# Two experts of a mixture in early and late passes, and TensorE's order in these passes written out

## The chip, the cores and the metric

One Trainium2 chip, one of its cores. The metric is the device time of the kernel in microseconds (us), the median over runs. The engines are called by their short names: PE (TensorE; PEld is its weight load), DVE (VectorE), ACT (ScalarE), POOL (GpSimd) and SP (SyncE, which issues most DMAs).

## The reference

The kernel computes an attention layer with a memory term and then a mixture of experts on its output. Shapes: batch B = 4, heads H = 8, sequence S = 576, head size D = 64, so 2304 tokens of width 512; E = 8 experts with hidden width 1024; float32.

```python
scores = scale * np.matmul(q, k.transpose(0, 1, 3, 2))      # causal mask, softmax
local = np.matmul(a, v)
q_p = phi(q)                                                # elu + 1
mem_out = einsum(q_p, M_prev) / (einsum(q_p, z_prev) + 1e-06)
x = (g * mem_out + (1 - g) * local), as (B * S, H * D)
...
noisy_logits = x @ w_gate + np.log1p(np.exp(x @ w_noise)) * noise
top2 = np.argpartition(-noisy_logits, 2, axis=1)[:, :2]     # weights: softmax over the two
for e in range(E):
    for k in range(2):
        mask = top2[:, k] == e
        h = np.maximum(x[mask] @ w1[e], 0.0)
        out[mask] += top2_w[mask, k, None] * (h @ w2[e])
```

Each token goes to two of the eight experts, and which ones is known only after its attention output has been computed.

## The kernel before

**Attention and routing.** attention() works through 20 chunks (4 batches of 5 chunks: four of 128 tokens and one of 64). The finished rows of x go to the DRAM scratch xall (line 643). For each chunk xt_logits (line 142) makes the gate's logits in three steps, f1 (transposes on PE), f2 (products) and f3 (transpose back). For each batch routing (line 176) yields a list of small steps on DVE and ACT; one of them, count, makes M, the mask of chosen experts, and places (line 237) counts positions with small matmuls on PE. A token's place gives its slot: every expert owns CAP = 608 slots. put (line 280) writes the token's row (token number, other slot, weight) into the DRAM table tab with an indirect DMA on POOL, two for each chunk. The last batch is routed in two parts, chunks 0 to 2 and 3 to 4; its tokens get slots from EARLY = 384 on (the offset dl, line 251), so the first 384 slots of every expert hold only tokens of batches 0 to 2. What is left of the routing when attention ends comes back as the list tail (line 797); its last step is rounds.

**Early rows of expert 0.** early() (line 837) runs when batch 2 has been routed: SP loads the first 384 rows of expert 0's part of tab into tabE, after all puts so far (line 842), and POOL gathers the 384 rows of x into xgE (line 850). xprep (line 852) turns such a tile on PE, and ACT and DVE split it into a high and a low part, xT.

**Experts.** All products run as three matmuls of split operands (high x high, high x low, low x high). Per expert there are 8 steps f of 128 hidden units. mm1 (line 907) makes the hidden tile for a step, with the relu on ACT (hTh, line 922) and the low part on DVE (hTl, line 923); mm2 (line 927) adds the step to the output banks y, one for each tile of slots: tiles 0 to 2 have 128 slots, tiles 3 and 4 have LATE = 112. Weights of a step are loaded by SP (load_w, lines 870 and 871, 2 x 256 KB, four buffers) and split by split_w (line 874): w1h on DVE, w1l on POOL (line 881), w2h on ACT, w2l on DVE. In the loop over steps, first(k + 1), the mm1 of the next step, comes ahead of the mm2 of step k.

The list of passes (line 945) sets the order: expert 0 with tiles 0 to 2 (early), expert 0 with tiles 3 and 4 (late; five of its eight steps take up splits that are still there: the order turn0 and the dict again), then experts 1 to 7 with all five tiles. In pass 0 the steps of tail are mixed in (tails) and the last puts go out, two after each step. When both lists are empty, load_tab (line 895) loads the whole table into tall, after all puts, and POOL gathers the late rows of expert 0 (xload(1)), which xprep turns on PE at the end of pass 0 (line 1074), ahead of pass 1.

From expert 1 on the rows of x are turned by DMA: xload gathers a tile into xg (five buffers), turn_x (line 996) separates the two 16-bit halves into pl (two buffers) with two copies on DVE and issues two DMA transposes on SP into trn; turned (line 1006) joins the halves on ACT and splits them into xT on ACT and DVE. xslot (line 1025) says in which step this is done: one tile a step in pass 1, joined four steps later.

**Results.** finish (line 1042) scales a tile by the routing weight. Rows of expert 0 are stored to the DRAM scratch ybuf only. For a later expert, yload gathers for each slot the row that the token's other expert has put there, if it had a lower number (g, with a memset on POOL ahead, line 814); finish adds it on DVE in one instruction, SP stores the sum to ybuf, and POOL scatters it to out (line 823). Such POOL and SP work is taken from the queue pq, two or three items a step.

**What sets the order.** The framework's planner orders the instructions of each engine anew, from the order in which they are written, with its own model of their durations; engines execute their queues in order. issue_after holds an instruction back behind another one. in_turn (line 726) fixes the order of the PE instructions that its function emits, behind those emitted by the one before; attention's steps all go through it, the experts' don't. The loop at line 1131 for more than CAP tokens of one expert runs zero times here.

Of the kernel before, what the change touches and what calls it, by code (L numbers as in the profile page):

```python
# [9 lines left out]
F32 = mybir.dt.float32  # L10
# [9 lines left out]
P = 128  # L20
# [26 lines left out]
def tile_attention_moe(ctx: ExitStack, tc: tile.TileContext, q, k, v, M_prev, z_prev, beta,  # L47
# [269 lines left out]


    def attention():
        with ExitStack() as c2:  # L320
# [405 lines left out]
            def in_turn(f):  # L726

                traced = nc.cur_bb.bb.instructions
                n_ = len(traced)
                f()  # L730
                for x_ in nc.cur_bb.bb.instructions[n_:]:
                    if x_.engine == mybir.EngineType.PE:
                        if "pe" in R:
                            tc.add_manual_dep(x_, R["pe"].name, mybir.DependencyInfo(
                                mybir.DependencyClass.NoSync, mybir.DependencyReason.DATA), reason="order of the steps")
                        R["pe"] = x_

            for u in range(NU + 2):
# [44 lines left out]
                for y, f in enumerate(ys):  # L783
                    in_turn(f)
                    if small:
                        in_turn(small.popleft())
                    while done * ny < (y + 1) * nx:
                        in_turn(xs[done])
                        done += 1
                        if small:  # L790
                            in_turn(small.popleft())
# [38 lines left out]
    tabE = ep.tile([P, 3, 4], I32, name="tabE")  # L830
# [6 lines left out]
    def early():  # L837
# [4 lines left out]
        after_puts(nc.sync.dma_start(out=tabE, in_=tab[0:EARLY].rearrange("(p t) c -> p t c", p=P)))  # L842
# [5 lines left out]
        for t in range(3):  # L848
            nc.vector.memset(R["xgE"][t], 0.0)
            gather_x(R["xgE"][t], tabE[:, t, 0:1], (B - 1) * S)  # L850
# [35 lines left out]
    def experts(tail):  # L886
        with ExitStack() as c3:
# [5 lines left out]
            tall = mp.tile([P, E, NT, 4], I32, name="tall")  # L893
# [13 lines left out]
            def mm1(ws, xT, tiles, odd=0):  # L907
# [5 lines left out]
                else:  # L913
                    cols = [(0, EARLY, "ab"[odd]) if tiles[0] < 3 else (EARLY, CAP, "ab"[1 - odd])]
                hp = [ps_h.tile([P, 512], F32, tag="h" + n_, name="h" + n_)[:, 0:c1_ - c0_] for c0_, c1_, n_ in cols]
                for c in range(4):
                    for i_, (w_, xi) in enumerate(((h1, 0), (h1, 1), (l1, 0))):
                        for (c0_, c1_, _), o in zip(cols, hp):
                            nc.tensor.matmul(o, w_[:, c, :], xT[xi][:, c, c0_:c1_],  # L919
# [25 lines left out]
            passes = [(0, [0, 1, 2]), (0, [3, 4])] + [(e, [0, 1, 2, 3, 4]) for e in range(1, E)]  # L945
# [10 lines left out]
            def tails(n):  # L956
                done = 0
                while done < n and tail:
                    if done and getattr(tail[0], "pe", False):
                        return  # L960
                    tail.popleft()()
                    done += 1

            def wload(k_):
                if k_ < len(steps) and k_ not in wr and k_ not in again:
                    p, f = steps[k_]
                    wr[k_] = load_w(mp, passes[p][0], turn0[f] if p == 1 else f, "m", 4)
# [7 lines left out]
            def first(k_):  # L975
                p, f = steps[k_]
                HT[k_] = mm1(ws[k_], XT[p], passes[p][1], f % 2 if p < 2 else 0)
# [3 lines left out]
            def xload(p):  # L981
# [4 lines left out]
                def one(t):  # L986
                    g = mp.tile([P, DM], F32, tag="xg", name="xg", bufs=5)
                    XG[p, t] = g
                    if len(XG) <= 5:
                        with tc.issue_after(R["hl"].ins):  # L990
                            nc.vector.memset(g, 0.0)
                    gather_x(g, tall[:, e, t, 0:1])
# [3 lines left out]
            def turn_x(xg, t):  # L996
# [5 lines left out]
                tr = R["turn", t] = mp.tile([P, 2, 4, P], U16, tag="trn", name="trn", bufs=4)  # L1002
# [3 lines left out]
            def turned(xT, t):  # L1006

                tr = R["turn", t]
# [4 lines left out]
                a_, b_ = slots_of(t)  # L1013
# [4 lines left out]
            def yload(p, t):  # L1018
                e = passes[p][0]
                g = mp.tile([P, DM], F32, tag="g", name="g", bufs=5)  # L1020
                G[p, t] = g
                with tc.issue_after(R["w1l"].ins):
                    gather_y(g, tall[:, e, t, 1:2], e * CAP)

            def xslot(p, f):

                if p == 0 and f + 3 >= NF:
                    p, f = 1, f - NF
                if p == 0 or p + 1 == NP_:
                    return  # L1030
                nx_ = passes[p + 1][1]
                begin = {1: [0, 1], 2: [2], 3: [3], 4: [4]} if p > 1 else {t - 3: [t] for t in range(5)}
# [175 lines left out]
```

## Time and profile before

| what | us |
|---|---|
| median of 3 runs | 771.13 |
| the three runs | 771.13, 771.33, 764.79 |
| profiled execution, first to last instruction (span) | 745.5 |
| what the median lies above that span | 25.6 |
| PE busy in the span | 700.6 (94%) |
| DVE, ACT, POOL busy | 422.5, 374.4, 347.3 |

The profiled execution's own time is known as its span only; the difference to the runs holds what lies around the span, and the scatter of runs. A profile counts an engine busy while an instruction runs; matmuls are pipelined, so their times overlap and the distance between starts is what a matmul costs. In the rows of stages below the columns are: the stage, its length, then for PE, PEld, DVE, ACT and POOL the busy time and in brackets the count of instructions, then the clock granted to PE as a share of full speed, the busy share of the DMA engines, and GB/s. In rows in order of time a bracket at the end is the engine's idle time just before, and what ended it.

### The profile page before, as it was taken

The numbers are of one execution on the slowest core, as the hardware profiler recorded it, in microseconds if no ns is written. First come the engines' busy times: TensorE is split into PE (matmuls) and PEld (weight loads), VectorE is DVE, ScalarE is ACT, GpSimd is POOL, SyncE is SP. The second block draws the span as 40 slices with busy tenths as digits, with TensorE's granted clock in tenths as the row PEclk, the third lists the DMA queues.
The fourth block names the chain that finished last, engine by engine and source line by source line (L and its number), as shares of the span: only waits on it lengthen the run. The fifth ranks groups of instructions, "written<-read, shape, count | busy, mean of one in ns | idle before, by whom it ended". The sixth has DMA issues, their size and how long they took to land. (4 is left out here: it accounts for less than half of the span.)

```text
span 745.5 us, 14446 instructions
## 1 busy us (share of the span) xinstructions
PE 700.6 (94%) x5166; PEld 603.4 (81%) x5166; DVE 422.5 (57%) x1073; ACT 374.4 (50%) x963; POOL 347.3 (47%) x368
## 2 busy tenths in 40 slices
PE   6999899999999878889999999999999999999993
PEld 4778777877878767777998898889889988988892
DVE  3766587678677669445555454455455354554312
ACT  4787788788888753155244153253153162253110
POOL 6513424632862516464533843833834744615402
PEclk7899999999999999989999999999999999999997
DMA  8764332251310047496593593684694695755201
GB/s 159 107 135 94 90 95 52 64 115 45 83 39 30 3 129 188 103 210 185 121 209 105 154 212 117 163 195 134 178 193 142 176 190 164 184 120 176 63 0 64
DMA packets 165919, 92.95 MB, mean 125 GB/s; under 512 B 110564, under 2 KB 145380, under 8 KB 165840
## 3 DMA queue, kind: packets, MB, share of 16 engines
q1 hardware_dynamic: 155760, 72.97, 40.5%
q0 software_dynamic: 10080, 18.98, 10.2%
q8 instruction: 43, 0.70, 0.4%
q14 instruction: 36, 0.29, 0.1%
HBM read 69.68 MB, written 22.54 MB: 124 GB/s over the span
## 5 line engine op out<-in xcount | busy, mean ns | idle before, releaser
L881 POOL TENSOR_TENSOR w1lm<-w1sm,w1hm 128x512 fp32r<-128x512 f32 x63 | 81.8, 1300 | 131.1 <-DVE w1hm L880 72.2
L932 PE MATMUL y<-w2hm,hTh 128*128 128x512 f32 (+1 forms) x310 | 122.9, 397 | 0.0
L932 PE MATMUL y<-w2hm,hTl 128*128 128x512 f32 (+1 forms) x310 | 122.4, 395 | 0.0
L932 PE MATMUL y<-w2lm,hTh 128*128 128x512 f32 (+1 forms) x310 | 122.0, 394 | 0.0
L922 ACT ACTIVATE hTh<-ha 128x304 fp32r<-128x304 f32 (+2 forms) x64 | 27.2, 426 | 157.1 <-PE ha L919 156.9
L882 ACT CAST w2hm<-w2sm 128x512 fp32r<-128x512 f32 x65 | 40.2, 620 | 102.1 <-PE y L932 102.1
L559 ACT ACTIVATE a<-sc,nb 128x128 f32<-128x128 f32 (+4 forms) x160 | 82.6, 531 | 11.4 <-DVE nb L538 6.7
L538 DVE TENSOR_REDUCE nb<-sc 128x1 f32<-128x384 f32 (+4 forms) x128 | 70.2, 557 | 27.7 <-PE sc L534 17.1
L883 DVE TENSOR_TENSOR w2lm<-w2sm,w2hm 128x512 fp32r<-128x512 f32 x65 | 49.0, 754 | 55.2 <-ACT w2hm L882 55.2
L880 DVE CAST w1hm<-w1sm 128x512 fp32r<-128x512 f32 x65 | 30.2, 464 | 78.3 <-PE hb L919 53.2
L919 PE MATMUL hb<-xTh,w1hm 128*128 128x304 f32 (+1 forms) x236 | 71.8, 304 | 0.0
L919 PE MATMUL ha<-xTl,w1hm 128*128 128x304 f32 (+1 forms) x236 | 71.8, 304 | 0.0
L919 PE MATMUL ha<-xTh,w1hm 128*128 128x304 f32 (+1 forms) x236 | 71.5, 303 | 0.0
L919 PE MATMUL ha<-xTh,w1lm 128*128 128x304 f32 (+1 forms) x236 | 71.1, 301 | 0.0
L919 PE MATMUL hb<-xTl,w1hm 128*128 128x304 f32 (+1 forms) x236 | 71.1, 301 | 0.0
L919 PE MATMUL hb<-xTh,w1lm 128*128 128x304 f32 (+1 forms) x236 | 70.8, 300 | 0.0
L932 PEld LDWEIGHTS y<-w2hm,hTl 128*128 128x128 f32 (+1 forms) x310 | 56.9, 184 | 15.6 <-DVE hTl L923 0.2
L932 PEld LDWEIGHTS y<-w2lm,hTh 128*128 128x128 f32 (+1 forms) x310 | 57.1, 184 | 12.1
L932 PEld LDWEIGHTS y<-w2hm,hTh 128*128 128x128 f32 (+1 forms) x310 | 57.0, 184 | 11.3
L577 PE MATMUL tpa<-identr,a 128*128 128x128 f32 x400 | 59.2, 278 | 5.1 <-ACT ll L170 3.4
L1001 DVE COPY pl<-xg 128x512 uint16<-128x512 uint16 x70 | 41.4, 639 | 38.1 <-DMA trn<-pl 26.2
L578 ACT COPY aT<-tpa 128x512 f32<-128x512 f32 x120 | 57.6, 519 | 6.4 <-PE tpa L577 4.4
(252 smaller groups left out, 1634.8 us busy)
## 6 DMA issues: line engine op xcount, KB each, us to landing
w1sm<-in_moe_w_dram SPq DMA_DIRECT2D x65, 256.0 KB, 3.2
w2sm<-in_moe_w_dram SPq DMA_DIRECT2D x65, 256.0 KB, 3.4
y_scratch<-o SPq DMA_DIRECT2D x21, 256.0 KB, 3.4
vt<-in_v_dram SPq DMA_DIRECT2D x16, 256.0 KB, 4.2
xall_scratch<-xr SPq DMA_DIRECT2D x16, 256.0 KB, 2.2
kn<-in_k_dram SPq DMA_DIRECT2D x15, 256.0 KB, 3.5
qn<-in_q_dram SPq DMA_DIRECT2D x15, 256.0 KB, 3.8
y_scratch<-o SPq DMA_DIRECT2D x14, 224.0 KB, 4.9
```

Source lines behind the costliest of these rows:

```text
L538: nc.vector.tensor_reduce(out=nb[:, t * nh:(t + 1) * nh], in_=cols[t] if nh == 2 else cols[t][:, 0, :], axis=AX.X, op=ALU.max, negate=True)
L559: nc.scalar.activation(a[:, o:o + w], s_, AF.Exp, bias=st["nb"][:, x_:x_ + 1], accum_out=d["den"][:, at:at + 1])
L577: nc.tensor.transpose(tp[:, x_ * P:(x_ + 1) * P], a[:, (g + x_) * P:(g + x_ + 1) * P], ident)
L578: nc.scalar.copy(aT[:, g:g + w, :].rearrange("p b t -> p (b t)"), tp[:, 0:w * P])
L880: nc.vector.tensor_copy(h1, a)
L881: R["w1l"] = lo.tensor_tensor(out=l1, in0=a, in1=h1.bitcast(F32), op=ALU.subtract)
L882: nc.scalar.copy(h2, b_)
L883: nc.vector.tensor_tensor(out=l2, in0=b_, in1=h2.bitcast(F32), op=ALU.subtract)
L919: nc.tensor.matmul(o, w_[:, c, :], xT[xi][:, c, c0_:c1_], start=(c == 0 and i_ == 0), stop=(c == 3 and i_ == 2))
L922: R["hh"] = nc.scalar.activation(hT[0][:, c0_:c1_], o, AF.Relu)
L932: nc.tensor.matmul(ys[t][0:b_ - a_], hT[hi][:, a_:b_], w_, start=(f == 0 and i_ == 0), stop=(f == FF // P - 1 and i_ == 2))
L1001: nc.vector.tensor_copy(pl[:, h_], xv[:, h_])
```

## The change

The passes become: expert 0 early, expert 1 early, expert 1 late, expert 0 late, then experts 2 to 7 with all tiles. tabE holds the early table rows of both experts, each loaded by a DMA of its own. Expert 1's early rows are gathered at the start of experts(), with a memset on POOL each; they and all late rows are turned by DMA with turn_x and turned, by a table of steps (begin, ready). The puts of the last batch are held behind the last of these gathers. xprep is used for the early rows of expert 0 only. The late passes take up two splits each from earlier steps (again). PE's order in passes 0 to 3, and in the steps of tail between them, is fixed through in_turn, which moves to the outer function; at most one PE step of tail is taken at five given points. Expert 1's results are scaled by ACT into tiles of their own (o1) and kept; in pass 4, when expert 0's rows are all stored, yload gathers them, combine adds them on DVE, SP stores and POOL scatters the sum. o has five buffers instead of six. In attention() only the name smalls is new, for lines that were there.

```diff
-    tabE = ep.tile([P, 3, 4], I32, name="tabE")
+    tabE = ep.tile([P, 2, 3, 4], I32, name="tabE")
...
-        after_puts(nc.sync.dma_start(out=tabE, in_=tab[0:EARLY].rearrange("(p t) c -> p t c", p=P)))
+        for e in range(2):
+            after_puts(nc.sync.dma_start(
+                out=tabE[:, e], in_=tab[e * CAP:e * CAP + EARLY].rearrange("(p t) c -> p t c", p=P)))
...
-            passes = [(0, [0, 1, 2]), (0, [3, 4])] + [(e, [0, 1, 2, 3, 4]) for e in range(1, E)]
+            passes = [(0, [0, 1, 2]), (1, [0, 1, 2]), (1, [3, 4]), (0, [3, 4])] + [(e, [0, 1, 2, 3, 4]) for e in range(2, E)]
+            NPART = 4
...
-            turn0 = [7, 6, 5, 1, 0, 4, 3, 2]
-            again = {NF + j: turn0[j] for j in range(5)}
+            turns = {2: [7, 6, 0, 1, 2, 3, 4, 5], 3: [2, 0, 3, 1, 4, 5, 6, 7]}
+            again = {2 * NF: 2 * NF - 1, 2 * NF + 1: 2 * NF - 2, 3 * NF + 1: 0, 3 * NF + 3: 1}
...
+            def tails(pe=False):
+                while tail:
+                    if getattr(tail[0], "pe", False):
+                        if not pe:
+                            return
+                        pe = False
+                    turn(tail.popleft())
+
+            def turn(f, *a):
+                if R["k"] <= NPART * NF:
+                    in_turn(lambda: f(*a))
+                else:
+                    f(*a)
...
+                    if p == 1:
+                        nc.gpsimd.memset(g, 0.0)
+                    elif len(XG) <= 5:
...
+                    if p == 1:
+                        R["xg1"] = gather_x(g, tabE[:, 1, t, 0:1], (B - 1) * S)
+                    else:
+                        gather_x(g, tall[:, e, t, 0:1])
...
+            for p, l in ((1, ((0, (0, 0), (0, 3)), (1, (0, 1), (0, 4)), (2, (0, 2), (0, 5)))),
+                         (2, ((3, (1, 1), (1, 3)), (4, (1, 2), (1, 5)))),
+                         (3, ((3, (1, 3), (1, 7)), (4, (1, 4), (2, 2)))),
+                         (4, ((0, (1, 5), (2, 4)), (1, (1, 7), (2, 6)), (2, (2, 1), (3, 0)), (3, (2, 3), (3, 2)),
+                              (4, (2, 5), (3, 4))))):
+                for t, s_, e_ in l:
+                    begin.setdefault(s_, []).append((p, t))
+                    ready.setdefault(e_, []).append((p, t))
...
+                    if e == 1:
+                        O[1, t] = mp.tile([P, DM], F32, tag=f"o1{t}", name=f"o1{t}")[0:n_]
+                        nc.scalar.activation(O[1, t], Y[p][t][0:n_], AF.Copy, scale=w_)
+                        continue
...
+            def combine(t):
+                o = O[1, t]
+                n_ = P if t < 3 else LATE
+                with tc.issue_after(R["hl"].ins):
+                    nc.vector.tensor_tensor(out=o, in0=o, in1=G[1, t][0:n_], op=ALU.add)
+                nc.sync.dma_start(out=y_rows(0, 1, t), in_=o)
+                scatter_out(o, tall[0:n_, 1, t, 2:3])
+
+            R["k"] = 0
+            for g in xload(1):
+                g()
...
             first(0)
-            tails(1)
+            tall = mp.tile([P, E, NT, 4], I32, name="tall")
+            tails(True)
             for k_, (p, f) in enumerate(steps):
...
-                turn = p == 0 and f == NF - 1
-                if turn:
-                    XT[1] = xt_tiles()
-                    for t in passes[1][1]:
-                        xprep(XT[1], XG[1, t], t, ps_y, f"y{t}")
-                if k_ + 1 < len(steps) and not turn:
+                if k_ + 1 < len(steps):
                     first(k_ + 1)
                 if f == 0:
                     Y[p] = y_tiles(tiles)
+                if k_ == 0:
+                    tails(True)
...
                     for t in tiles:
-                        mm2(ws[k_], HT[k_], [t], Y[p], f)
-                        if p == 0:
-                            tails(16)
...
+                        turn(mm2, ws[k_], HT[k_], [t], Y[p], f)
+                        tails()
+                if p < 2:
+                    tails(k_ in (0, 3, 4))
+                    with tc.issue_after(R["xg1"].ins):
+                        for _ in range(2):
+                            if puts:
+                                puts.popleft()()
+                    if "tab" not in R and not tail and not puts:
                         R["tab"] = True
...
                         load_tab()
+                        pq.extend(xload(2) + xload(3) + xload(4))
+                if f == 0:
+                    if p == NPART:
+                        pq.extend(lambda t=t: yload(1, t) for t in range(NT))
+                        pq.extend(lambda t=t: combine(t) for t in range(NT))
```

## Rows read from the trace of the kernel before

**Rows 1.** Busy time by stage, core 0; after PEclk the DMA share and GB/s
```profile
280.00:290.00 10.00, 10.00 (x60) 8.97 (x59) 9.04 (x31) 4.23 (x11) 6.22 (x6) 1.00 0.84 218
290.00:300.00 10.00, 7.97 (x44) 6.91 (x43) 9.43 (x38) 1.49 (x4) 5.91 (x5) 1.00 0.61 173
320.00:340.00 20.00, 17.94 (x98) 15.23 (x99) 12.63 (x24) 11.62 (x21) 10.66 (x10) 0.84 1.01 247
380.00:420.00 40.00, 40.00 (x231) 35.85 (x230) 21.37 (x40) 15.97 (x31) 19.55 (x20) 1.00 0.62 160
```

**Rows 2.** Waits of TensorE: for what, us in total, times, longest
```profile
PE tpm L855 <- DMA xg<-xall_scratch,tall: 5.2, 2, 3.0
...
PE pp L240 <- DVE M L222: 2.0, 1, 2.0
PE y L932 <- DVE hTl L923: 1.8, 1, 1.8
```

**Rows 3.** TensorE in order of time: start us, us, line, out<-in, count, idle
```profile
279.03 0.46 PE L149 MATMUL tpx<-identr,xr 64*128 64x64 f32 x4 [1.06 <-DVE xr L639]
...
303.67 0.39 PE L932 MATMUL y<-w2hm,hTh 128*128 128x512 f32 x1
...
305.73 0.51 PE L919 MATMUL ha<-xw,w1hm 128*128 128x384 f32 x2
...
307.83 0.39 PE L932 MATMUL y<-w2hm,hTh 128*128 128x512 f32 x1
...
312.04 0.39 PE L932 MATMUL y<-w2hm,hTh 128*128 128x512 f32 x1
...
324.77 0.27 PE L919 MATMUL hb<-xTh,w1hm 128*128 128x224 f32 x1
...
335.60 0.40 PE L932 MATMUL y<-w2hb,hTh 128*112 128x512 f32 x1
...
342.02 0.39 PE L932 MATMUL y<-w2ha,hTh 128*112 128x512 f32 x1
...
343.41 0.27 PE L919 MATMUL hb<-xTh,w1hm 128*128 128x224 f32 x1
...
344.74 0.40 PE L932 MATMUL y<-w2hm,hTh 128*112 128x512 f32 x1
...
346.13 0.27 PE L919 MATMUL ha<-xTh,w1hm 128*128 128x224 f32 x1
...
353.88 0.31 PE L919 MATMUL ha<-xTh,w1hm 128*128 128x304 f32 x1
...
360.70 0.30 PE L919 MATMUL ha<-xTh,w1hm 128*128 128x304 f32 x1
```

**Rows 4.** GpSimd in order of time, 269 to 313 us
```profile
269.34 0.53 POOL L898 IOTA tall<- 32x160 int32 x1
282.26 1.03 POOL L282 DMA_INDIRECT tab_scratch<-rows,six  x1 [12.38 <-DVE rows L196]
...
312.62 1.04 POOL L809 DMA_INDIRECT xg<-xall_scratch,tall  x1 [4.42 <-DMA tall<-tab_scratch]
```

**Rows 5.** VectorE in order of time, 293 to 338 us
```profile
293.41 1.58 DVE L880 CAST w1hm<-w1sm 128x512 fp32r<-128x512 f32 x1
...
335.76 0.76 DVE L1001 COPY pl<-xg 128x512 uint16<-128x512 uint16 x2 [2.63 <-DMA trn<-pl]
...
337.64 0.38 DVE L923 SCALAR_TENSOR_TENSOR hTl<-ha,hTh 128x224 fp32r<-128x224 f32 x1
```

**Rows 6.** The page's costliest groups: count, busy us, mean ns, idle before
```profile
L881 POOL TENSOR_TENSOR w1lm<-w1sm,w1hm 128x512 fp32r<-128x512 f32 x63 | 81.8, 1300 | 131.1 <-DVE w1hm L880 72.2
...
L883 DVE TENSOR_TENSOR w2lm<-w2sm,w2hm 128x512 fp32r<-128x512 f32 x65 | 49.0, 754 | 55.2 <-ACT w2hm L882 55.2
L880 DVE CAST w1hm<-w1sm 128x512 fp32r<-128x512 f32 x65 | 30.2, 464 | 78.3 <-PE hb L919 53.2
...
L1001 DVE COPY pl<-xg 128x512 uint16<-128x512 uint16 x70 | 41.4, 639 | 38.1 <-DMA trn<-pl 26.2
```

More of the change, by code (lines that the diff above doesn't have):

```diff
@@ L316, in routing, with in_turn @@
         return steps
+    def in_turn(f):
+        traced = nc.cur_bb.bb.instructions
+        n_ = len(traced)
+        f()
+        for x_ in nc.cur_bb.bb.instructions[n_:]:
+            if x_.engine == mybir.EngineType.PE:
+                if "pe" in R:
+                    tc.add_manual_dep(x_, R["pe"].name, mybir.DependencyInfo(
+                        mybir.DependencyClass.NoSync, mybir.DependencyReason.DATA), reason="order of the steps")
+                R["pe"] = x_
     def attention():
@@ L724, in on_chunk, with smalls @@
                     late_consts()
[L726 to L736, printed above, removed]
+            def smalls():
+                if small:
+                    in_turn(small.popleft())
             for u in range(NU + 2):
@@ L905, in xt_tiles, with mm1 @@
                 return [mp.tile([P, 4, CAP], F32R, tag="xT" + s_, name="xT" + s_, bufs=2) for s_ in "hl"]
[L907 removed]
+            def mm1(ws, xT, tiles, odd=0, at=0):
                 h1, l1 = ws[0], ws[1]
@@ L976, in first @@
                 p, f = steps[k_]
-                HT[k_] = mm1(ws[k_], XT[p], passes[p][1], f % 2 if p < 2 else 0)
+                turn(lambda: HT.update({k_: mm1(ws[k_], XT[p], passes[p][1], k_ % 2, EARLY if p == 3 else 0)}))
             pq = deque()
@@ L1001, in turn_x, with turned @@
                     nc.vector.tensor_copy(pl[:, h_], xv[:, h_])
-                tr = R["turn", t] = mp.tile([P, 2, 4, P], U16, tag="trn", name="trn", bufs=4)
+                tr = R["turn", p, t] = mp.tile([P, 2, 4, P], U16, tag="trn", name="trn", bufs=4)
                 for h_ in range(2):
                     nc.sync.dma_start_transpose(out=tr[:, h_], in_=pl[:, h_])
-            def turned(xT, t):
-                tr = R["turn", t]
+            def turned(p, t):
+                if p not in XT:
+                    XT[p] = {2: XT[1], 3: XT[0]}[p] if p in (2, 3) else xt_tiles()
+                xT = XT[p]
+                tr = R["turn", p, t]
                 xf = mp.tile([P, 4, P], F32, tag="xf", name="xf", bufs=2)
@@ L1085, in experts @@
                     for t in tiles:
-                        mm2(ws[k_], HT[k_], [t], Y[p], f)
-                        if p == 0:
-                            tails(16)
-                if turn:
-                    first(k_ + 1)
-                if p == 0:
-                    tails(16)
-                    for _ in range(2):
-                        if puts:
-                            puts.popleft()()
-                    if "tab" not in R and (f == 5 or not tail):
+                        turn(mm2, ws[k_], HT[k_], [t], Y[p], f)
@@ L1114, in experts @@
                         pq.extend(lambda t=t: yload(p, t) for t in tiles)
-                if f == 4 and p > 0:
+                if f == 4 and p >= NPART - 1:
                     pq.extend(xload(p + 2))
-                for _ in range(3 if f == 0 else 2):
-                    if pq:
+                for _ in range(3 if f == 0 or p == NPART else 2):
+                    if pq and (p > 1 or R.get("tab")):
                         pq.popleft()()
@@ L1131, in experts @@
             with tc.For_i(0, over, 1):
-                zt = mp.tile([P, DM], F32, tag="zt", name="zt")
+                zt = mp.tile([P, DM], F32, tag="pl", name="zt", bufs=2)
                 nc.vector.memset(zt, 0.0)
```

91 lines of the change are left out of this document (33 added, 58 removed).

## The prediction, made blind

> **What bounds the kernel now.** I read the busy time by stage first. From 380 us on TensorE is busy 40.00 of 40 us at granted clock 1.00, with the other engines near half [rows 1]: experts 2 to 7 are bound by TensorE, the change leaves them alone, and nothing is to be had there. In the stretch where expert 0 runs it isn't so: 7.97 of 10 us from 290, and 17.94 of 20 us from 320 at a mean granted clock of 0.84, so part of that stretch ran at the lower of the two levels (1.2 instead of 2.4 GHz) just after TensorE had stood still [rows 1]. The waits of TensorE name three causes: 5.2 us for the gathers of expert 0's late rows (xg, turned on TensorE), 2.0 us for M (the count of chosen experts, in the routing of the last chunks), 1.8 us for hTl [rows 2].
>
> TensorE in order of time gives what each cost with its slow clock [rows 3]. An early step (384 slots) is mm2 303.67 to 305.73 = 2.06 us and mm1 to 307.83 = 2.10, together 4.16. A late step (224 slots) is mm1 343.41 to 344.74 = 1.33 and mm2 to 346.13 = 1.39, together 2.72. A whole step is 353.88 to 360.70 = 6.82.
> - The gathers: two mm2 from 312.04 would have ended at 316.16, the next mm1 began at 324.77: 8.6 us.
> - hTl: mm2 and mm1 of a late step from 335.60 would have ended at 338.32, the next mm2 began at 342.02: 3.7 us, twice the wait.
> - M: 2.0 us [rows 2].
>
> Sum 14.3 us. This is all that the change can win, since attention stays and the end of the kernel stays.
>
> **What it removes.** The late rows' gathers were issued at 312.62, after GpSimd had waited 4.42 us for tall [rows 4], and TensorE wanted them some 3 us later. Now 8 early steps of expert 1 lie in between and the late pass of expert 1 begins only after 16 early steps: 279.5 + 16 x 4.16 is 346 us. Were tall read 5 us later than before, some 25 us of cover would be left for gather, transpose and split. So the 8.6 us go, with the 8 transposes on TensorE that lay inside them. If that cover were gone, the whole 8.6 would be back.
>
> M: places() was put by the planner inside mm1 of step 4; in the new fixed order it stands behind mm2 of step 3, over 2 us of matmuls further on. I count the 2.0 us as gone, and put 0.6 us back for it and for f2, which now follows f1 by only one mm1 (bounds 0 and 2.0, the old wait; nearer to 0, as the cover is larger than the wait).
>
> hTl at 335: VectorE stood 2.63 us for a pl buffer that a DMA transpose was still reading, then did other work, and hTl came at 337.64 [rows 5]. It was the pass in which five tiles were turned within 22 us. In the new table pass 0 turns three tiles one step (4.16 us) apart, passes 1 to 3 turn nine, mostly two short steps apart. So this one goes too, but its kind can come back: see below.
>
> **What it adds.** Cutting expert 1: 4.16 + 2.72 - 6.82 = 0.06 us a step, 0.5 for eight [rows 3]. f1 (0.46 us) filled a gap of 1.06 us ahead of the first mm1 [rows 3]; behind that mm1 it costs 0.5.
>
> Weights: four passes of 8 steps with 4 reused need 28 loads, before it was three passes with 5 reused, 19. Nine more, each 512 KB and a split: 1.30 us on GpSimd, 0.46 + 0.75 on VectorE [rows 6]. Passes 2 and 3 last 16 x 2.72 = 43.5 us and hold 12 splits, 15.6 us of GpSimd and 14.5 of VectorE: each fits beside TensorE. The DMA: 28 loads over 110 us are 134 GB/s, with gathers, stores and transposes an estimated 200 from the sizes of their tiles; 320 to 340 us shows 247 GB/s at a share of 1.01 [rows 1]. So nothing, while the loads run ahead; without that lead a step of 2.72 us with a load wants 193 GB/s for weights alone.
>
> Early gathers: GpSimd does three memsets and three gathers behind the iota at 269.34, where it had nothing to do for 12.38 us [rows 4]; the puts that follow wait for the last of them. At 1.04 us a gather [rows 4] and a memset of at most as much this is 6 us: nothing. SP issues one more read of tab, 6 more transposes in pass 0; ahead of them in its queue stand only weight loads with steps to spare.
>
> VectorE in pass 0: it is busy 18.47 of the 20 us from 280 [rows 1], and gets three tiles more: two copies of 0.64 us each, 3.8 us, and three subtractions, by w2lm's row 0.75 each, 2.3 us [rows 6]. 6.1 us don't fit into 1.5. They fit into the whole pass of 33 us if the order is right. This is the step that I trust least. The sum takes one stall of the hTl kind for passes 0 to 3, 3.7 us with its slow clock. Bounds: none, and by the old density (one stall in five tiles turned) 12/5 x 3.7 = 8.9; the spacing is about double, so nearer to one than to 2.4.
>
> Expert 1's results go through ScalarE into o1, and a sum on VectorE in pass 4 takes the place of the old fused one: 5 instructions in 55 us of cover, nothing. If GpSimd waits for the stores of y there, only splits with steps to spare are queued behind.
>
> **The sum.** 14.3 - 0.5 - 0.5 - 0.6 - 3.7 = 9.0 us. The profiled execution spans 745.5 us, 25.6 below the median of 771.1 (19.3 below the fastest run, 764.8); what lies around the span I take as unchanged. 745.5 - 9.0 = 736.5; 771.1 - 9.0 = 762.1, rounded to 762.0, 1.2% less. A difference of 1% (7.7 us) is about what a measurement of this kernel can tell.
>
> **A rule weighed.** The cast of w1 has a mean of 0.46 us and took 1.58 at 293.41 [rows 5, 6], while GpSimd was in its subtraction of 1.30. The Trainium skill (SBUF — State Buffer, "Who interferes with whom") says that a copy or cast of VectorE in its two-port mode and a GpSimd instruction take one shared port pair as a lock, and the second waits the other out in full. The trace agrees: 0.46 and at most 1.30 hold the 1.58. By that rule the pl copies, which are copies too, would speak against the change: it is the worse half of the first rival.
>
> **Rivals.**
> - VectorE becomes the bound of pass 0. For: 18.47 of 20 us. Price: 6.1 - 1.5 = 4.6 us, doubled by the slow clock as the 1.8 became 3.7: 9.2; 771.1 - (14.3 - 1.6 - 9.2) = 767.6. If each of the six copies also waits out a GpSimd subtraction, 6 x 1.3 = 7.8 more, 12.4 in all without doubling: 770.8. Against: part of the 18.47 is weight splits done ahead, which can wait.
> - The early gathers aren't early: xg's buffers lie where attention's tiles lay, and the gathers or the transposes behind them come only when pass 0 is well on. Then VectorE, in order, waits for xg, and TensorE pays the 8.6 us of before once more: 771.1 - (9.0 - 8.6) = 770.7. For: the same wait of 5.2 us [rows 2]. Against: 12 idle us on GpSimd.
> - Slower: the stalls on transposes repeat. Each tile's copies wait in VectorE's queue for a pl buffer or a gather, hTl stands behind, and each such stall costs 3.7 us. There are 12 tiles; with four stalls (14.8) the win of 12.7 is gone, 773.2, with six it is 780.6. For: the DMA share of 1.01 when transposes and weights met [rows 1], and the page's 26.2 us of waiting for trn<-pl in the same copies [rows 6]; TensorE's order is now fixed, so it can't fill a gap with other work. Against: the wider spacing.
>
> **How the numbers follow.** Forecast with none to two stalls: 758.4, 762.1, 765.8: 0.54. VectorE bound, 767.6 to 770.8: 0.13. Late gathers, 770.7: 0.09. Repeated stalls, 773 to 781: 0.16. What I don't see (the planner orders all other engines anew): 0.08, mostly slower. Faster by over 1% (below 763.4): 0.48 of the first case and 0.02 of the unseen, 0.50. Slower by over 1% (above 778.8): 0.11 of the repeated stalls and 0.06 of the unseen, 0.17. Within 1% the rest, 0.33. The range goes from 755 (no stall, 3 us for the scatter of runs) to 776 (four to five stalls).
>
> **What would show it.** Right: no wait of TensorE for xg between 279 and 390 us; mm1 of expert 2 (304 columns) beginning at some 394 us: 279.5 + 16 x 4.16 + 16 x 2.72 - 1.39 (the mm2 that follows it) + 1.0 (f1 to rounds) is 389 without stalls, and 4.3 for those that I count; PEclk 1.00 in all stages of 20 us but one; expert 1's gathers issued before 277. Wrong: several waits for hTl or for a trn tile with PEclk below 0.9 in more than one stage, or gathers into xg for expert 1 after 285. The prediction falls if the stretch up to expert 2 shrinks by less than 4 us.

## The result, and the profile after

The median is 761.95 us (758.81 to 766.59, 12 runs) against 770.37 us (764.79 to 773.5, 12 runs) of the kernel before: 8.4 us less, a ratio of 0.9898 with a 95% interval from 0.9876 to 0.9921. The forecast was 9.0 us less.

The profiled execution took 760.25 us with a span of 758.5, so 1.7 us lie around the span and not 25.6. The trace says where the rest of those 25.6 lay. TensorE in order of time, kernel after (start us, us, line, out<-in, count, idle before and what ended it):

```profile
129.62 1.11 PE L589 MATMUL tpa<-identr,a 128*128 128x128 f32 x4 [4.64 <-issue]
...
202.31 1.11 PE L589 MATMUL tpa<-identr,a 128*128 128x128 f32 x4 [6.82 <-issue]
...
276.60 0.32 PE L160 MATMUL tpl<-xTlh,wgs 128*32 128x128 f32 x1 [6.95 <-ACT xTlh L152]
...
303.15 0.44 PE L923 MATMUL ha<-xw,w1ha 128*128 128x384 f32 x1 [0.68 <-ACT xw L864]
304.14 0.44 PE L923 MATMUL ha<-xw,w1ha 128*128 128x384 f32 x1 [0.54 <-DVE xw L865]
...
372.29 0.27 PE L923 MATMUL ha<-xTh,w1hm 128*128 128x224 f32 x1
...
417.07 0.30 PE L923 MATMUL ha<-xTh,w1hm 128*128 128x304 f32 x1
```

Three stops of 4.6 to 7.0 us stand inside attention, which the change leaves alone, and the first mm1 begins at 303.15 instead of just after 279.03 [rows 3]. The trace of before that the prediction was read from has no such stop. Its span of 745.5 us fits a chip without them (run 1: 745.34 us), the three times beside it fit a chip with them (runs 5 to 8). For the kernel before this rests on times alone: no trace of it on a chip with stops is on record. One plain consequence: the two traces have to be compared from the first mm1 on.

From there: mm1 of expert 2 (304 columns) begins 417.07 - 303.15 = 113.9 us after the first mm1. Before, it began at 401.68, some 122.3 after it. On top comes that the mm2 which follows this mm1 belongs to a late step now (1.39 us) and to a whole step of 3.43 before, so the stretch is 8.4 + 2.0 = 10.4 us shorter. From the first mm1 to the last matmul it is 444.0 us after and 453.8 before.

The page's slices of TensorE and of its granted clock (40 slices, tenths), kernel after:

```profile
PE   6999897999699958999999999999999999999993
...
PEclk8899998999899989999999999999999999999998
```

The dips are those of attention; from the seventeenth slice on nothing dips before the last. Busy time by stage in the new expert stretch (columns as in [rows 1]):

```profile
320.00:340.00 20.00, 19.75 (x102) 17.24 (x101) 18.45 (x69) 11.10 (x20) 9.05 (x9) 1.00 0.64 168
340.00:360.00 20.00, 20.00 (x101) 18.02 (x100) 15.12 (x17) 6.88 (x12) 12.89 (x12) 1.00 0.79 220
360.00:380.00 20.00, 20.00 (x116) 17.93 (x115) 13.85 (x27) 11.52 (x22) 10.78 (x9) 1.00 1.09 251
380.00:400.00 20.00, 19.67 (x129) 17.00 (x128) 18.38 (x30) 14.03 (x28) 11.94 (x10) 1.00 1.04 242
```

TensorE is busy 19.67 us or more of every 20 from 320 on, at clock 1.00, where before a stage had 17.94 at 0.84 [rows 1]. VectorE's 18.45 of 20 beside TensorE's 19.75 is the reading to keep: a share of 92% did not make it the bound. Part of such a share need not be work either: the paragraph on the shared port shows 5.06 us for two copies of 0.43. The waits of TensorE from 279 us on (us in total, times, longest), kernel after:

```profile
PE y L936 <- DVE hTl L927: 1.4, 3, 0.8
...
PE ha L923 <- ACT xw L864: 0.7, 1, 0.7
...
PE ha L923 <- DVE xw L865: 0.5, 1, 0.5
...
PE hb L923 <- DVE hTl L927: 0.2, 1, 0.2
```

The waits for xg (5.2) and M (2.0) of [rows 2] are gone, hTl is down from one wait of 1.8 to small ones, and two waits for xw at the first mm1 are new. GpSimd in order of time, kernel after, shows the two sets of gathers:

```profile
290.62 1.00 POOL L812 DMA_INDIRECT xg<-xall_scratch,tabE  x1 [0.28 <-POOL xg L1002]
...
294.50 1.01 POOL L812 DMA_INDIRECT xg<-xall_scratch,tabE  x1 [0.18 <-issue]
...
345.98 1.05 POOL L812 DMA_INDIRECT xg<-xall_scratch,tall  x1 [4.45 <-DMA w2sm<-in_moe_w_dram]
```

Expert 1's early gathers run 12.5 to 8.7 us ahead of the first mm1. The first late gather again stands behind a wait of 4.45 us, as before (4.42, [rows 4]). The profile names a weight load; more likely it was the table's read, issued at 341.86, 4.1 us ahead of the gather (before: at 309.59, 3.0 us ahead). The difference is who wants the rows. After, it is TensorE at 372.29, 26.3 us later. Before, it stood from 314.27 on, 1.7 us later (the prediction has some 3), as this row of before shows:

```profile
317.31 0.78 PE L855 MATMUL tpm<-identr,xg 128*128 128x128 f32 x4 [3.04 <-DMA xg<-xall_scratch,tall]
```

The 26.3 us are not idle cover, though. VectorE's last split of these rows, kernel after:

```profile
371.07 0.62 DVE L1038 TENSOR_TENSOR xTl<-xf,xTh 128x448 fp32r<-128x448 f32 x1
```

It ends at 371.69, 0.6 us ahead of the pass that reads it (run 9: 346.56 against 348.67, 2.1 us). The table of steps and the queues spread the turning over the whole stretch.

### The profile page after: what moved, and what is told of

Read it like the earlier page. It is cut to its first block, busy times and chain, and to the rows that moved or that the text cites. A ratio compares the mean times of both kernels' runs of the same rounds, so it can differ in the third digit from the quotient of the medians.

```text
span 758.5 us, 14553 instructions
## 1 busy us (share of the span) xinstructions
PE 704.0 (93%) x5158; PEld 606.0 (80%) x5158; DVE 448.6 (59%) x1092; ACT 385.5 (51%) x981; POOL 359.3 (47%) x380
## 5 line engine op out<-in xcount | busy, mean ns | idle before, releaser
L886 POOL TENSOR_TENSOR w1lm<-w1sm,w1hm 128x512 fp32r<-128x512 f32 x72 | 93.0, 1296 | 116.4 <-DVE w1hm L885 55.3
L936 PE MATMUL y<-w2hm,hTl 128*128 128x512 f32 (+1 forms) x310 | 122.3, 395 | 1.4 <-DVE hTl L927 1.4
L887 ACT CAST w2hm<-w2sm 128x512 fp32r<-128x512 f32 x74 | 45.7, 619 | 95.2 <-PE y L936 89.4
L888 DVE TENSOR_TENSOR w2lm<-w2sm,w2hm 128x512 fp32r<-128x512 f32 x74 | 61.1, 826 | 55.2 <-ACT w2hm L887 51.6
L923 PE MATMUL hb<-xTh,w1hm 128*128 128x304 f32 (+2 forms) x224 | 68.6, 306 | 0.2 <-DVE hTl L927 0.2
L923 PE MATMUL ha<-xTl,w1hm 128*128 128x304 f32 (+2 forms) x224 | 68.2, 304 | 0.0
L923 PE MATMUL hb<-xTl,w1hm 128*128 128x304 f32 (+2 forms) x224 | 68.0, 303 | 0.0
L923 PE MATMUL ha<-xTh,w1hm 128*128 128x304 f32 (+2 forms) x224 | 67.8, 303 | 0.0
L923 PE MATMUL hb<-xTh,w1lm 128*128 128x304 f32 (+2 forms) x224 | 67.7, 302 | 0.0
L923 PE MATMUL ha<-xTh,w1lm 128*128 128x304 f32 (+2 forms) x224 | 67.6, 302 | 0.0
L611 PE MATMUL avT<-aT,vt 128*64 128x128 f32 (+1 forms) x960 | 61.7, 272 | 0.0
```

What stands on the lines that cost most here:

```text
L611: nc.tensor.matmul(o_[k_ * 64:(k_ + 1) * 64, h0 // 2, 0:n], CH[c0 + j]["v"][:, h0 + k_, :], r_, start=(j == 0), stop=(j == i))
L886: R["w1l"] = lo.tensor_tensor(out=l1, in0=a, in1=h1.bitcast(F32), op=ALU.subtract)
L887: nc.scalar.copy(h2, b_)
L888: nc.vector.tensor_tensor(out=l2, in0=b_, in1=h2.bitcast(F32), op=ALU.subtract)
L923: nc.tensor.matmul(o, w_[:, c, :], xT[xi][:, c, c0_ - at:c1_ - at], start=(c == 0 and i_ == 0), stop=(c == 3 and i_ == 2))
L936: nc.tensor.matmul(ys[t][0:b_ - a_], hT[hi][:, a_:b_], w_, start=(f == 0 and i_ == 0), stop=(f == FF // P - 1 and i_ == 2))
```

## The experiments

The first four kernels ran on one chip, the next four on a second, the last three on a third, each group beside its own runs of the kernel before.

**1. The kernel before once more** (no edit, one execution).

> The kernel before, unchanged, for a second profile. The changed kernel's span of 758.5 us lies only 1.7 us below the time of the same execution (760.25), while the profile of before spans 745.5 and its runs took some 770. Theory: the profile of before caught an execution without the three stops that the changed kernel's trace shows in attention (4.6, 6.8 and 7.0 us, and slow clock behind each), and ordinary executions of both kernels have them. Then this profile spans 765 to 770 us, shows three idle stretches of TensorE of 4 to 7 us between 120 and 280 us, and behind attention the same waits as before: 5.2 us for xg, about 2 each for M and hTl. Rival: the change itself brought the stops; then this profile has none and spans about 745.

Measured: 745.34 us, span 743.5; the runs of before on this chip have a median of 745.83 (13 runs). No stop in attention; TensorE waited 2.0 us for M, 2.8 for xg and 3.1 for hTl in the expert stretch. So 1.8 us lie around the span here too, and the expectation of 765 to 770 fell. By itself this run fits the rival, that the change brought the stops; runs 5 and 9 settle that. The single waits differ from those of [rows 2], but not their sum: from the first mm1 to the last matmul it is 454.1 us here and 453.8 in the first trace.

**2. The order of TensorE in the four passes left to the planner.**

```diff
-                if R["k"] <= NPART * NF:
-                    in_turn(lambda: f(*a))
-                else:
-                    f(*a)
+                f(*a)
```

> The changed kernel with TensorE's order in the passes of experts 0 and 1 left to the planner, all else as changed. Theory (the gain is the cover that expert 1's early steps give to the late rows): 0 to 3 us slower than the changed kernel, at 762 to 765 us, for one wait of about 2 us for M if places moves forward again. Rival (the gain is the fixed order): most of the 8 us is lost, 768 to 771.

Measured: 735.01 us, ratio 0.9855 (0.9809 to 0.9901), four waits for hTl of 0.24 to 0.30. The changed kernel did not run on this chip; beside its ratio of 0.9898 elsewhere the gain is there in full without the fixed order. The order is not its source.

**3. The five tiles of expert 2 turned close together**, as before the change, in the late pass.

```diff
-(4, ((0, (1, 5), (2, 4)), (1, (1, 7), (2, 6)), (2, (2, 1), (3, 0)), (3, (2, 3), (3, 2)), (4, (2, 5), (3, 4))))
+(4, ((0, (2, 5), (3, 1)), (1, (2, 6), (3, 2)), (2, (2, 7), (3, 3)), (3, (3, 0), (3, 4)), (4, (3, 1), (3, 5))))
```

> The changed kernel with the five tiles of the first whole expert turned one short step apart from (2,5) on and joined four steps later, as the kernel before did it, instead of two steps apart from (1,5) on. Theory of the prediction (stalls on hTl come from the density of turned tiles): one or two stalls of 3.7 us come back in pass 3, 764 to 770 us, with waits of TensorE for hTl of 2 us and more after 385 us. Rival (the density does nothing; the wait of before came from the gathers and transposes being late as a whole): 761 to 763.

Measured: 736.62 us, ratio 0.9885 (0.9841 to 0.9929). The waits of TensorE, this kernel:

```profile
PE y L936 <- DVE hTl L927: 1.9, 3, 1.0
PE hb L923 <- DVE hTl L927: 0.6, 1, 0.6
```

That is 2.5 us of waits, where the changed kernel has 0.9 to 1.7 (runs 9 and 5), but none is above 1.0 us. Density alone doesn't bring back the stall of 3.7 us.

**4. The passes of before, with the fixed order and the new places of the routing steps.** The list of passes, the tables and the gathers are those of before; in_turn and tails are those of the change.

```diff
+                if R["k"] <= 2 * NF:
+                    in_turn(lambda: f(*a))
```

> The kernel before with its own passes, but with TensorE's order fixed in the two passes of expert 0 and the steps of tail taken at the points of the changed kernel. Theory: the 2.0 us for M go and the waits for the late rows stay, as nothing covers them: 767 to 770 us. Rival (order and placing are the gain): 761 to 764.

Measured: 743.65 us, ratio 0.9979 (0.9944 to 1.0014). The wait for M is gone, and TensorE in order of time shows the one for the gathers larger than the 5.2 of [rows 2]:

```profile
315.43 1.11 PE L855 MATMUL tpm<-identr,xg 128*128 128x128 f32 x4 [4.65 <-DMA xg<-xall_scratch,tall]
318.24 1.12 PE L855 MATMUL tpm<-identr,xg 128*128 128x128 f32 x4 [1.70 <-DMA xg<-xall_scratch,tall]
```

M alone is worth nothing that can be measured: the late rows are what TensorE meets next, and it meets them that much earlier. Their first gather comes 35.2 us after the last transposes of early rows began (310.72 - 275.48), as before (312.62 - 277.37), and from the first mm1 to the last matmul it is 453.95 us, as in both traces of before. The times alone (743.65 against 745.83) would not exclude a gain of 2 us.

**5. The changed kernel once more**, beside the next three.

> The changed kernel, unchanged, beside the kernel before on a chip on which neither e1 to e4 nor the kernel before show the stops in attention. Theory (the stops belong to the chip, and the change saves TensorE waits behind attention only): span 733 to 736 us, no stop in attention, ratio 0.986 to 0.990, the same 8 to 10 us as before. Rival (a slower attention hides part of the gain or makes part of it): the difference moves by more than 3 us from 8.4.

Measured: 759.45 us, before 769.06, ratio 0.9894 (0.9846 to 0.9942). Stops of 3.17, 5.21 and 8.26 us in attention, at the places of the first three rows of after. The expectation of no stops fell; that of the gain held, 9.6 us. The time of before beside it, 769.06, fits stops there too.

**6. Expert 1's early gathers written behind the first mm1.**

```diff
-            for g in xload(1):
-                g()
...
             first(0)
+            with tc.issue_after(R["hl"].ins):
+                for g in xload(1):
+                    g()
```

> The changed kernel with the three early gathers of expert 1 (and their memsets) written behind the first mm1 and held until its hTl exists, so that they are issued some 10 us later, with the table of steps as it was. The prediction's rival priced late gathers at 8.6 us: VectorE, in order, waits for xg ahead of its first pl copy, hTl stands behind it, and TensorE pays. By that price 743 to 746 us here. Other theory (the lag of three steps and the order of the queues give slack enough, as splits and hTl of two more steps stand ahead of the copies): within 2 us of the changed kernel.

Measured: 760.06 us, ratio 0.9878 (0.9827 to 0.9929). The hold in the edit did not bind: the hTl of the first mm1 came at 307.01, and the first gather ran 1.2 us ahead of the first mm1 (300.43 against 301.65). It did move, from 12.5 us ahead, and the waits of TensorE stayed at 0.7 us or less each. Eleven us later cost nothing that shows: VectorE's copies of these rows stand 28.4, 18.6 and 14.7 us ahead of pass 1 here, 28.6, 18.6 and 14.7 in the changed kernel. The table of steps sets them, not the gathers.

**7. The copies into pl for passes 1 to 4 on ScalarE instead of VectorE.**

```diff
-                    nc.vector.tensor_copy(pl[:, h_], xv[:, h_])
+                    (nc.scalar.copy if p <= NPART else nc.vector.tensor_copy)(pl[:, h_], xv[:, h_])
```

> The changed kernel with the pl copies of its passes 1 to 4 (24 copies) on ScalarE instead of VectorE, where one of them took 4.7 us beside GpSimd's subtractions. Theory A (VectorE's queue and its collisions with GpSimd are what is left of TensorE's waits): the waits of TensorE for hTl go, 1 to 2 us faster than the changed kernel. Theory B (the long copies lie in slack): within 0.3%, and hTh may come later by ScalarE's longer copies of 0.8 us.

Measured: 758.98 us, ratio 0.9894 (0.9840 to 0.9948), the changed kernel's own 0.9894. The waits for hTl fall from 1.7 us (run 5) to 0.6, and one of 1.4 us for hTh comes, which ScalarE makes:

```profile
PE y L936 <- ACT hTh L926: 1.4, 1, 1.4
PE y L936 <- DVE hTl L927: 0.4, 1, 0.4
```

**8. The read of the whole table four steps later in the program**, and the late tiles' steps with it.

```diff
-                         (2, ((3, (1, 1), (1, 3)), (4, (1, 2), (1, 5)))),
-                         (3, ((3, (1, 3), (1, 7)), (4, (1, 4), (2, 2)))),
+                         (2, ((3, (1, 3), (1, 5)), (4, (1, 4), (1, 6)))),
+                         (3, ((3, (1, 5), (1, 7)), (4, (1, 6), (2, 2)))),
...
-                    if "tab" not in R and not tail and not puts:
+                    if "tab" not in R and k_ == 8:
```

> The changed kernel with load_tab and with it all gathers of late rows four steps (16.6 us) later, and the steps in which the late tiles of experts 1 and 0 are turned moved back by two steps. Theory (some 25 us of cover stand between the table and the late pass of expert 1): still covered, within 3 us of the changed kernel. Rival (the cover is nearly used up by gathers, transposes and splits in a row): TensorE waits at the start of pass 2 for xT, 5 to 12 us slower.

Measured: 760.88 us, ratio 0.9893 (0.9857 to 0.9928). TensorE in order of time:

```profile
371.26 0.37 PE L923 MATMUL ha<-xTh,w1hm 128*128 128x224 f32 x1 [0.47 <-ACT xTh L1037]
373.43 0.37 PE L923 MATMUL ha<-xTl,w1hm 128*128 128x224 f32 x1 [1.80 <-DVE xTl L1038]
```

The run did not test what it was made for. The read was issued 36.9 us after the first mm1 (338.86 - 301.99), in the changed kernel 38.7 (341.86 - 303.15): it comes 2 to 3 us behind the last put in both, whatever its place in the program, and so it never came 16.6 us later. What did move is the turning of the tiles, by some 7 us (the first copy of late rows 55.2 us after the first mm1, 48.2 in the changed kernel), and that alone brought 2.3 us of waits. It agrees with the 0.6 to 2.1 us by which the rows are ready ahead of their pass. The median did not move (759.45 in run 5).

**9 and 10. The changed kernel and the free order side by side**; 10 is the edit of 2.

> The changed kernel once more, beside the kernel with the free order (next) and on its chip. Both earlier ratios were 0.9894 to 0.9898. Expected here: 0.990 (0.987 to 0.993) against the kernel before, whether or not the chip is one on which attention stops. Theory A (the fixed order of TensorE costs nothing once no tile comes late): this kernel and the next agree within 0.3%. Theory B (a fixed order costs, since TensorE can't fill a gap with other work): this one is 2 to 4 us (0.3 to 0.5%) longer.

> The change with TensorE's order in the four passes left to the planner. It gave 0.9855 against the kernel before (0.9809 to 0.9901) where the changed kernel gave 0.9894 and 0.9898 elsewhere. Theory A: the difference is chance, 0.989 to 0.990 here. Theory B: it is 0.985 to 0.987 again and the interval lies below that of the changed kernel's. The difference, if there is one, should stand ahead of the first mm1 (f1 in the gap there, 0.5 us) and in the waits for hTl (1.6 us in all with the fixed order).

Measured on a chip without stops, before 746.15 us (17 runs): the changed kernel 735.98 (734.35 to 737.26, 5 runs), ratio 0.9855 (0.9813 to 0.9897); the free order 733.35 (732.13 to 736.88, 6 runs), ratio 0.9828 (0.9788 to 0.9868). TensorE in order of time, the changed kernel here:

```profile
278.19 0.60 PE L860 MATMUL tpm<-identr,xw 128*128 128x128 f32 x4
...
279.46 0.44 PE L923 MATMUL ha<-xw,w1ha 128*128 128x384 f32 x1 [0.68 <-ACT xw L864]
280.44 0.45 PE L923 MATMUL ha<-xw,w1ha 128*128 128x384 f32 x1 [0.54 <-DVE xw L865]
...
282.97 0.62 PE L923 MATMUL hb<-xw,w1hb 128*128 128x384 f32 x2
...
348.67 0.27 PE L923 MATMUL ha<-xTh,w1hm 128*128 128x224 f32 x1
...
393.45 0.30 PE L923 MATMUL ha<-xTh,w1hm 128*128 128x304 f32 x1
```

and with the free order:

```profile
276.41 0.60 PE L860 MATMUL tpm<-identr,xw 128*128 128x128 f32 x4
...
278.07 0.46 PE L149 MATMUL tpx<-identr,xr 64*128 64x64 f32 x4 [1.06 <-DVE xr L651]
278.45 0.90 PE L923 MATMUL ha<-xw,w1ha 128*128 128x384 f32 x2
...
282.25 0.51 PE L923 MATMUL hb<-xw,w1hb 128*128 128x384 f32 x2
...
391.87 0.30 PE L923 MATMUL ha<-xTh,w1hm 128*128 128x304 f32 x1
```

The change is worth 10.2 us on this chip. No stop stands in attention here, so the change did not bring the stops. The free order's median is 2.6 us lower still, the lowest of this study, but the intervals overlap, and the rows don't put the difference into the expert passes. Attention is through 1.8 us earlier in the profiled execution of 10 (its last transposes, tpm, begin at 276.41 and not at 278.19), and from there to expert 2 it is 115.5 us against 115.3. From tpm to the mm1 of the second step (hb) the free order takes 5.84 us here, at a mean granted clock of 0.86 from 276 to 288 us, and 4.29 in run 2 (276.56 to 280.85); the fixed order takes 4.78, with f1 behind the first mm1 and two waits for xw.

**11. The late gathers held back until expert 1's early pass is nearly over.**

```diff
-                         (2, ((3, (1, 1), (1, 3)), (4, (1, 2), (1, 5)))),
-                         (3, ((3, (1, 3), (1, 7)), (4, (1, 4), (2, 2)))),
-                         (4, ((0, (1, 5), (2, 4)), (1, (1, 7), (2, 6)), (2,
+                         (2, ((3, (1, 5), (1, 6)), (4, (1, 5), (1, 6)))),
+                         (3, ((3, (1, 6), (2, 1)), (4, (1, 7), (2, 3)))),
+                         (4, ((0, (1, 7), (2, 4)), (1, (2, 0), (2, 6)), (2,
...
-                    if pq and (p > 1 or R.get("tab")):
-                        pq.popleft()()
+                    if pq and k_ >= NF + 5:
+                        if p > 1:
+                            pq.popleft()()
+                            continue
+                        with tc.issue_after(R["hl"].ins):
+                            pq.popleft()()
```

> The late gathers of experts 1 and 0 and all that stands on them held back to the last two steps of expert 1's early pass, some 18 us later than the changed kernel issues them (by TensorE's clock: 61 instead of 43 us after the first mm1). The late pass then has some 7 us of cover, where the kernel before took 12.2 us from the gather to the matmuls (312.62 to 324.77). Theory of the cover (the gain is the distance between the gathers and the pass that reads them): TensorE waits 4 to 8 us for expert 1's late rows (xTh or xTl) ahead of the third pass, the clock falls after it, the time goes up by 6 to 12 us on the changed kernel, ratio 0.997 to 1.005. Rival (the gain is in the cut of expert 1 and in the spread of the turned tiles): a wait of under 2 us, ratio still 0.989 to 0.992.

Measured on the chip of 9 and 10: 750.70 us (10 runs), ratio 1.0061 (1.0029 to 1.0093), 14.7 us above the changed kernel. GpSimd's first two late gathers, then TensorE in order of time, then the stage in which it stands:

```profile
338.99 1.05 POOL L812 DMA_INDIRECT xg<-xall_scratch,tall  x1
343.21 1.02 POOL L812 DMA_INDIRECT xg<-xall_scratch,tall  x1 [3.17 <-DVE xg L1005]
```

```profile
357.41 0.56 PE L923 MATMUL ha<-xTh,w1hm 128*128 128x224 f32 x1 [9.87 <-ACT xTh L1037]
...
406.92 0.30 PE L923 MATMUL ha<-xTh,w1hm 128*128 128x304 f32 x1
```

```profile
340.00:360.00 20.00, 10.03 (x48) 8.63 (x47) 7.13 (x14) 5.54 (x9) 7.35 (x8) 0.77 0.69 168
```

Everything else of the change is still there (expert 1 cut, early gathers, spread of pass 1, fixed order; the first two tiles of expert 2 are begun later with the rest), and the kernel is slower than before. The late pass begins 8.7 us later than in 9 (357.41 against 348.67), and the passes from there to expert 2 take 49.5 us instead of 44.8: a lower clock behind the stop (0.77 in that stage) and waits for hTl of up to 1.2 us. Together 13.5 of the 14.7 us. The theory of the cover holds; its price was set too low.

## Why the prediction came out right

**The time.** 8.4 us less against 9.0 forecast in the result and 9.6 in run 5, both with stops, 10.2 in run 9, without. All lie within the first case's own span (none to two stalls). That 761.95 stands so near 762.0 is luck: several terms were off, and their errors cancel, as told below.

**The gathers of the late rows, 8.6 us: right in mechanism, and shown.** No wait for xg or xT stands in passes 0 to 3 of the changed kernel; in run 11, with the cover taken away, 9.9 us of wait and 14.7 us of time come back. "Some 25 us of cover" is 26.3 by the trace (345.98 to 372.29), with other parts: in run 9 the first gather came 8.5 us later than before, where the prediction allowed 5 for the table's read, and the pass 2.7 us later than its 346. Run 11 also says how much of it is needed at most: 338.99 to 357.41, 18.4 us from the first gather to the matmuls through transposes by DMA, 14.2 of them behind the second gather, which waited 3.17 us for a memset that the edit holds on VectorE. The kernel before took 12.2 from 312.62 to 324.77 with TensorE's own transposes [rows 3, 4]. So 8 us or more could be spared if the tiles were turned at once; as the table of steps stands, 0.6 to 2.1 us are left, and the later turning of run 8 ran into them. The step "if that cover were gone, the whole 8.6 would be back" was too small, since it took the old, shorter way.

**M, 2.0 us: gone, and by itself worth nothing that shows.** Run 4 removes it without the cover, and the stretch from the first mm1 to the last matmul stays at 454 us. The sum is valid because the gathers' wait goes with it; as separate terms the two were not independent.

**The fixed order as the source or the risk: neither.** Runs 2 and 10 keep the gain without it. Its price at the first mm1 is the 0.5 us that the prediction gives f1: 4.78 us from tpm to hb in run 9 against 4.29 in run 2. The matmuls wait for xw, 0.68 and 0.54 us, while f1, free to go ahead, used to stand in that gap [rows 3]. A further cost of the order is not shown.

**The new stall of 3.7 us: mis-sized.** It was the largest of the terms that the change adds. What came in run 9, by the distance between starts, is 1.5 us from 338.85 to 344.48 (5.63 against 4.16 for an early step) and 0.6 at 376.10 behind a wait of 0.33 for hTl: 2.1 us, at clock 1.00. In the trace of the result three waits for hTl make it 2.2. The reason given, the density of turned tiles, was not borne out by run 3. The wait on transposes is still there. In run 9 VectorE stood for a buffer that one was reading, as long as the 2.63 of [rows 5], and ScalarE stood 5.36 us for a transpose's result, until 338.64. VectorE, then TensorE in order of time:

```profile
338.95 0.76 DVE L1020 COPY pl<-xg 128x512 uint16<-128x512 uint16 x2 [2.71 <-DMA trn<-pl]
```

```profile
341.61 0.50 PE L936 MATMUL y<-w2hm,hTh 128*128 128x512 f32 x1 [0.47 <-ACT hTh L926]
...
342.76 0.50 PE L936 MATMUL y<-w2hm,hTl 128*128 128x512 f32 x1 [0.42 <-DVE hTl L927]
```

The hTh of this step, whose mm1 was through by 337, stood in ScalarE's queue behind that joining and ran at 341.07; the hTl that needs it came after (342.15). So what decides is whether a due hTh or hTl is queued behind such a wait. That reading rests on the order of the rows; no run moved that alone.

**What lies around the span, 25.6 us: wrong, and without effect on the difference.** 1.7 to 1.8 us lie around it. The rest goes with chips that have the stops, and falls on both kernels about alike (runs 5 and 9: 23.5 us for the changed kernel, 22.9 for the one before), so subtracting from the span and adding back gave the right time. It would have failed for a change to attention.

**The position of expert 2.** "Some 394 us" is 393.45 in run 9, on a chip as that of the first profile. The sum is met with other parts. The 4.3 us above the 389 without stalls had been counted as 3.7 for a stall and 0.6 for M and f2. They are 1.0 in the first mm1 (3.12 us against 2.10, with the wait of 0.54 for xw), the 2.1 of the stalls above, and 1.2 in pieces that no row of waits names.

**The rivals.**
- VectorE as the bound of pass 0: it reached 18.45 of 20 us and TensorE 19.75. The price of 4.6 us came from adding the new work to a stage that held work which could move. Run 7 takes the copies off it and gains nothing.
- Early gathers not early: half true, as the second memset waited 5.4 us for a buffer that attention's scores used. They were still 8.7 us ahead of the first mm1, and run 6 shows that eleven us later costs nothing. By the letter a sign of being wrong came, "gathers into xg for expert 1 after 285" (290.62 in the result): attention there ended 23.7 us later than in run 9, where they begin at 271.89. The price of 8.6 us was borrowed from a wait with 1.7 us of cover; here there are 33.
- Repeated stalls: four waits for hTl in the whole stretch of the result, none above 0.8 us.

**The rule of the shared port.** VectorE and GpSimd in order of time, kernel after, first VectorE:

```profile
351.31 5.06 DVE L1020 COPY pl<-xg 128x512 uint16<-128x512 uint16 x2 [0.85 <-issue]
```

```profile
352.28 3.80 POOL L886 TENSOR_TENSOR w1lm<-w1sm,w1hm 128x512 fp32r<-128x512 f32 x3
```

Two copies that take 0.43 us each by the median of their kind took 5.06 together, and GpSimd ran three subtractions back to back under them. By the Trainium skill (SBUF — State Buffer, "Who interferes with whom") one of the two waits out the other's instruction; the trace agrees, with three in a row where the prediction counted one of 1.30 us for a copy. TensorE was busy 20.00 of 20 us in that stage, so it cost nothing there. The rule held, and the rival built on it did not.

## What to carry to other kernels

A wait on a gather is removed by distance: find the step that needs the rows, count back the whole way from gather to split (14 to 18 us here), and put work of the same kind that needs nothing new in between. Then look at when the last split ends, not only at the gather: the steps in which the tiles are turned can use the distance up (0.6 us were left of 26.3). Before pricing waits as a sum, ask whether one stands right behind another: taking only the first away (M in run 4) moves the engine up to the second. A busy share of 92% beside TensorE's 99% need not be a bound; whether something due is queued behind a wait is what to look for.

## What the hardware showed beyond that

The same program takes some 746 us on two of the chips and some 769 on others (kernel before: medians 745.83 and 746.15 against 769.06 and 770.37). In the changed kernel, where traces of both forms are on record, the first mm1 begins at 279.46 us in run 9 and at 303.15 in the result. Of these 23.7 us, 18.4 are three stops of TensorE in attention, at 125.0 to 129.6, 195.5 to 202.3 and 269.7 to 276.6 us; behind them the granted clock is lower (0.50 from 129.6 to 134 us, 0.65 from 202.3 to 208). ScalarE and SyncE stand with TensorE, VectorE runs three short instructions in each stop, and the DMA engines move 1 to 5 GB/s. ScalarE in order of time, kernel after, at the second:

```profile
201.67 0.58 ACT L453 COPY qf<-tpq 128x512 f32<-128x512 f32 x1 [7.60 <-remote]
```

and GpSimd at the same time, at the end of its ten puts of a batch:

```profile
198.85 0.90 POOL L282 DMA_INDIRECT tab_scratch<-rows,six  x1 [0.30 <-issue]
200.06 0.90 POOL L282 DMA_INDIRECT tab_scratch<-rows,six  x1 [0.30 <-issue]
202.32 0.61 POOL L464 CAST qh<-qf 128x512 fp32r<-128x512 f32 x1 [1.37 <-issue]
```

ScalarE goes on near the tenth put of each burst: 0.8 us ahead of it, 0.7 us behind its end, and at its end (275.96). For most of these waits the profile names no releaser. The puts alone are not it: in run 9 ten puts run from 182.90 to 195.6 us, and TensorE is busy 13.11 of the 14 us from 182. Why a chip does this stays open; no run moved the puts.
